# Sliding-window attention with a three-way maxout block: differences of hidden blocks issued later, normalising on VectorE, part of the weights' low parts on GpSimd

## The chip, the cores and the metric

The kernel runs on one core of one Trainium2 chip. A core has five engines, each with an instruction queue of its own that is worked off in order: PE (TensorE, matmuls; PEld are its weight loads), DVE (VectorE), ACT (ScalarE), POOL (GpSimd) and SP (SyncE, here only DMA issues). The metric is the device time of one execution in microseconds (us); less is better.

## The reference

q, k and v are 8 batches x 8 heads x 576 positions x 64; the block behind the attention has 4608 tokens, d_model 512 and d_ff 768.

```python
scores = scale * np.matmul(q, k.transpose(0, 1, 3, 2))
bias = slopes[:, None, None] * (-np.abs(rel).astype(np.float32))[None, :, :]
mask = (rel >= 0) & (rel < window)            # window = 128
scores = np.where(mask, scores + bias[None], -1000000000.0)
attn = np.exp(scores - np.max(scores, axis=-1, keepdims=True))
attn = attn / (np.sum(attn, axis=-1, keepdims=True) + 1e-09)
x = np.matmul(attn, v)                        # heads side by side: 4608 x 512
h = np.maximum(np.maximum(x @ w1, x @ w2), x @ w3)
return (h @ w_out).astype(np.float32)
```

## The kernel before

*Attention.* A task is one batch and one pair of heads, a step one block of 128 queries of a task (five blocks, the last of 64). `score` adds the bias on DVE (L289, with the row's minimum into `st`), and ACT takes the exponential into a tile `p` with the row sums (L293). `sums_of` adds 1e-9 to the sums (L302) and takes reciprocals (L305), both on DVE, for two blocks at a time. `normalise` (L312) multiplies each of the two heads' halves of `p` by the reciprocal of its row, on ACT. `turn` transposes `p` on PE (L321), ACT copies it out (L325, L334) and POOL cuts it into two triangles (L335, L339); `mix` multiplies with v (L361).

*The block behind it* is one level of a two-by-two fast matrix product in seven products of sums and differences of blocks (k = 0 to 6). A unit is one product k of one group g of 128 columns; each batch has 9 groups of the first layer (three matrices for each of three parts p of d_ff) and 2 groups of the last, 77 units. Matrices are split into a high part of reduced precision and the rest, the low part, and a product is three matmuls per 128 rows: six matmuls for a unit of the first layer, nine for one of the last (L510). `unit` takes the result out of PSUM: k below 3 by an ACT copy (L519), the others in `put` on DVE (L468, L473 to L476, L459) or ACT (L457, L470). Three PSUM banks go round, so that a unit needs the bank that was taken out three units earlier.

*Weights.* `preparing` reads twelve groups of weights once, converts them from words (L136 to L144), forms sums (L158), and splits each of the seven blocks of 256 columns in `part`: the high part on ACT (L168), the low part on DVE (L169). Groups 0 to 8 are stored to DRAM (L171, on SP's queue) and streamed back for each later batch (L221, on POOL's queue).

*Hidden blocks.* When a part p of the hidden layer is ready, `factors_h` forms its sums and differences on DVE (`sub`, L391) and splits them (`cut`): the high part by ACT (L387), the low part by POOL, or by DVE for p = 2 and k below 2 (L388). `factors_x` does the same for the attention's output. These calls are put into a list with a time in units by `later`, and `unit` calls what is due before its own matmuls.

*Order.* `at` gives each call a time in steps; the calls are recorded sorted by it. The units of a batch are spread over the steps of the next batch's attention. A scheduler then sets each engine's order from the recorded program, and buffers are few, so that a late instruction in one queue holds back all that stand behind it there.

Of the kernel before, what the change touches and what calls it, by code (L numbers as in the profile page):

```python
# [8 lines left out]
F32 = mybir.dt.float32  # L9
# [3 lines left out]
AF = mybir.ActivationFunctionType  # L13
ALU = mybir.AluOpType
# [15 lines left out]
def attention_maxout_kernel(  # L30
# [11 lines left out]
    nc = tc.nc  # L42
# [43 lines left out]
        out=prev, in_=prev, pattern=[[1, P]], compare_op=ALU.is_gt, fill=0.0,  # L86
# [59 lines left out]
    def blocks(g):  # L146

        (l0, h0), (l1, h1) = [[x.bitcast(F32) for x in words(g, j)] for j in range(2)]
        a, b = slice(0, W), slice(W, 2 * W)
        return l0[:, a], h0[:, b], h1[:, a], h1[:, b], l1[:, a], h0[:, a], l1[:, b], l0[:, b]  # L150
# [9 lines left out]
    def part(g, k):  # L160
        src = blocks(g)[k]
        if g < 9:
            if k in (0, 4):
                place(g, k // 4)
            t = wts[g, k // 4][:, k % 4]
        else:
            t = ow[k][:, g - 9]
        nc.scalar.copy(out=t[:, 0], in_=src)  # L168
        nc.vector.tensor_tensor(out=t[:, 1], in0=src, in1=t[:, 0].bitcast(F32), op=ALU.subtract)  # L169
        if g < 9 and k in (3, 6):  # L170
            nc.sync.dma_start(keep[g][k // 4], wts[g, k // 4].bitcast(F32))  # L171

    def place(n, a):
        wts[n, a] = wt_p.tile([P, 4 - a, 2, W], F32R, name=f"wt{a}")
# [8 lines left out]
    def preparing():  # L183
        fetch(0)
        fetch(1)
        for n, g in enumerate(g_order):
            for j in range(2):
                convert(g, j)
                yield
            sums(g)  # L190
            yield
            for k in range(7):
                while g < 9 and not ahead(g, k // 4):
                    yield True
                part(g, k)
                yield
            if n + 2 < NG:
                fetch(g_order[n + 2])
# [108 lines left out]
    def normalise(t, i):  # L307
        n = rows[i]
        st, two = stats[t, i // 2]
        for a, p in enumerate(two):  # L310
            for j in range(2):
                nc.scalar.activation(p[:n, j], p[:n, j], AF.Copy, scale=st[:n, 2, a, j:j + 1])  # L312

    def turn(s):
        pt = ps_t.tile([P, 2, 2, P], F32, name="pt")
# [63 lines left out]
    def later(when, what, *args):  # L379
        todo.append((when, what, args))  # L380
        todo.sort(key=lambda x: x[0])
# [3 lines left out]
    def split(out, src, e):  # L385
        hi, lo = out
        nc.scalar.copy(out=hi, in_=src)  # L387
        e.tensor_tensor(out=lo, in0=src, in1=hi.bitcast(F32), op=ALU.subtract)  # L388

    def sub(out, x, y):  # L390
        nc.vector.tensor_tensor(out=out, in0=x, in1=y, op=ALU.subtract)  # L391
# [28 lines left out]
    def factors_h(b, p, ij, when):  # L420
        b00, b01, b10, b11 = [hq.get((p, x)) for x in ((0, 0), (0, 1), (1, 0), (1, 1))]

        def cut(k, src):
            if p < 2:
                if p == 0:
                    hs[b, k] = hs_p.tile([P, 2, 2, C], F32R, name="hs")
                t = hs[b, k][:, p]
            else:
                if k in (0, 2, 4, 5):
                    hs[b, "at"] = hs_p.tile([P, 2, 2, C], F32R, name="hs2", bufs=4)  # L430
                t = hs[b, k, 2] = hs[b, "at"][:, k in (1, 3, 6)]
            split((t[:, 0], t[:, 1]), src, nc.vector if p == 2 and k < 2 else nc.gpsimd)

        if ij == (0, 0):
            t = hq["t", p] = t_p.tile([P, C], F32, name="t")
            sub(t, b01, b00)
            later(when, cut, 0, b00)
            later(when, cut, 1, t)
        elif ij == (1, 1):
            t = hq["t", p]  # L440
            later(when, sub, t, b11, t)
            later(when, sub, b01, b11, b01)
            later(when, cut, 2, t)
            later(when, cut, 3, b11)
        elif ij == (1, 0):
            t = hq["t", p]
            later(when, cut, 5, b01)
            later(when, cut, 4, b10)
            later(when, sub, b10, b10, t)
            later(when, cut, 6, b10)  # L450

    def put(b, g, ij, ps, e, when):
        i, j = ij
        if g >= 9:
            o = t_p.tile([P, C], F32, name="t")
            if e is None:
                nc.scalar.copy(out=o, in_=ps)  # L457
            else:
                nc.vector.tensor_tensor(out=o, in0=ps, in1=e, op=ALU.add)  # L459
            m = i * W + (g - 9) * P  # L460
            nc.sync.dma_start(outT[m:m + P, b * S + j * C:b * S + (j + 1) * C], o)
            return
        p, w = divmod(g, 3)
        if w == 0:
            hq[p, ij] = hq_p.tile([P, C], F32, name="hq")
        h = hq[p, ij]
        if w and e is None:
            nc.vector.tensor_tensor(out=h, in0=ps, in1=h, op=ALU.max)  # L468
        elif e is None:
            nc.scalar.copy(out=h, in_=ps)  # L470
        elif w:
            s = t_p.tile([P, C], F32, name="t")
            nc.vector.tensor_tensor(out=s, in0=ps, in1=e, op=ALU.add)  # L473
            nc.vector.tensor_tensor(out=h, in0=s, in1=h, op=ALU.max)  # L474
        else:
            nc.vector.tensor_tensor(out=h, in0=ps, in1=e, op=ALU.add)  # L476
        if w == 2:
            factors_h(b, p, ij, when + 1)
# [54 lines left out]
    for t, (b, hp) in enumerate(tasks):  # L533
        for i in range(NB):
            s = t * NB + i + shift[b]
            if i == LOAD_I and t + 2 < len(tasks):
                at(s - 0.4, load, t + 2)
            if i == NB - 1 and t + 1 < len(tasks):
                at(s - 0.4, load_v, t + 1)
            if i == 0 and 0 < t < NP:  # L540
                at(s - 1, slopes, t)
            c = s - (t * NB + i) % 2

            if s == c:
                at(c + LAG_T + 0.02, turn, t * NB + i)
                at(c + 0.03, products, t * NB + i)
            at(s + 0.04, score, t, i)
            if i % 2 or i + 1 == NB:
                at(s + 0.9, sums_of, t, i)
                at(s + 1.3, normalise, t, i)  # L550
            e = t * NB + next(min(e + 1, NB - 1) for e in GROUPS if e >= i)
            at(e - e % 2 + shift[b] + LAG_X + 0.01, mix, t, i)

    ready = [n_steps * (b + 1) - 2 + LAG_X + 0.05 + shift[b] for b in range(B)]
    when = ready[0]
    for b in range(B):
# [4 lines left out]
        for u in range(77 * b, 77 * b + 77):  # L561
            if u == 77 * b + 63 and b + 1 < B:
                when = max(when, ready[b + 1])
# [53 lines left out]
```

## Time and profile before

| | us |
|---|---|
| median of 3 runs | 849.85 (846.66 to 851.54) |
| the profiled execution | 846.03 |
| its span | 844.3 |
| PE busy | 780.3 (92%) |
| DVE busy | 570.0 (68%) |
| ACT busy | 544.5 (64%) |
| POOL busy | 310.3 (37%) |

All that follows is read from one profiled execution. Times are us from the start of the span unless marked ns. A row such as "A <- B" says that A's engine stood idle until B was done. A group's busy time leaves out overlaps, so it can be less than its count times its mean. Tile names stand as out<-in, with the program's numbers left out: `hq` are hidden blocks, `hs` their split parts and also the raw weights, `xk` and `xs` the same for the attention's output, `t` temporaries, `wt` and `ow` split weights, `ps_m` the PSUM banks of the units, `ps_s` those of the scores.

### The profile page before, as it was taken

How to read it: one execution, taken by the hardware profiler on the slowest of the kernel's cores; microseconds unless marked ns; L12 is line 12 of the kernel's file. 1: busy time of each engine (PE TensorE's matmuls, PEld its weight loads, DVE VectorE, ACT ScalarE, POOL GpSimd, SP SyncE). 2: the span in 40 equal slices, each digit the busy share in tenths (PEclk: the TensorE clock that was granted, in tenths of full speed). 3: DMA queues.
4: the chain of work that ended last, by engine and by line, in shares of the span. 5: the costliest groups of instructions: out<-in, count | busy, mean ns of one | idle time of the engine just before them, and what ended most of it. 6: DMA issues, size and time to landing. Idle time of an engine off the chain costs nothing.

```text
span 844.3 us, 17942 instructions
## 1 busy us (share of the span) xinstructions
PE 780.3 (92%) x6272; PEld 674.3 (80%) x6272; DVE 570.0 (68%) x1830; ACT 544.5 (64%) x1790; POOL 310.3 (37%) x544
## 2 busy tenths in 40 slices
PE   4767778799999999999999999999999999999997
PEld 2335666589888988888888988889888988889897
DVE  5788989996666845775557845775657846583552
ACT  6898888876666856676556756675657756642332
POOL 1212141442354415452345415451345415440431
PEclk9865989799999999999999999999999999999999
DMA  6742568673887558873787558873787557764851
GB/s 230 278 168 70 220 230 305 210 257 125 262 277 249 195 171 261 277 253 118 239 273 252 196 175 267 275 255 110 245 281 240 194 187 244 230 223 153 296 205 56
DMA packets 43401, 184.78 MB, mean 219 GB/s; under 512 B 4784, under 2 KB 13744, under 8 KB 34096
## 3 DMA queue, kind: packets, MB, share of 16 engines
q0 software_dynamic: 18144, 115.61, 41.7%
q1 hardware_dynamic: 25024, 67.97, 22.8%
q8 instruction: 49, 0.80, 0.4%
q14 instruction: 40, 0.33, 0.1%
q10 hardware_dynamic: 144, 0.07, 0.0%
HBM read 157.68 MB, written 25.95 MB: 217 GB/s over the span
## 4 chain that ended last, share of the span: by engine, by line
PE 68%; DVE 8%; issue 8%; POOL 6%; ACT 6%; DMA 3%; SPq 0%; POOLq 0%; ACTq 0%; DVEq 0%
PE ps_m L510 53%; PE ps_x L361 6%; PE ps_s L259 5%; PE pt L321 4%; POOL hs L388 3%; DMA wt<-keep 2%; POOL pp L339 1%; POOL pp L335 1%; ACT p L293 1%; ACT hs L387 1%; DVE hs L158 1%; DVE t L473 1%; DMA hs<-in_w_all 1%; DVE hs L144 1%; DVE xs L388 1%
## 5 line engine op out<-in xcount | busy, mean ns | idle before, releaser
L510 PE MATMUL ps_m<-xs,wt 128*128 128x288 f32 x3024 | 440.8, 302 | 19.9 <-DVE hq L476 7.6
L510 PEld LDWEIGHTS ps_m<-xs,wt 128*128 128x128 f32 x3024 | 414.6, 191 | 46.6 <-issue 12.2
L519 ACT COPY t<-ps_m 128x288 f32<-128x288 f32 x264 | 101.2, 392 | 92.3 <-PE ps_m L510 91.9
L335 POOL TENSOR_SCALAR_AFFINE_SELECT pp<-pr 128x256 f32<-128x256 f32 (+1 forms) x128 | 53.9, 421 | 263.0 <-ACT pr L334 175.9
L510 PE MATMUL ps_m<-hs,ow 128*128 128x288 f32 x1008 | 144.5, 299 | 3.2 <-POOL hs L388 2.4
L293 ACT ACTIVATE p<-s,st 128x128 f32<-128x128 f32 (+1 forms) x320 | 126.7, 399 | 27.9 <-DVE st L289 27.2
L510 PEld LDWEIGHTS ps_m<-hs,ow 128*128 128x128 f32 x1008 | 136.0, 188 | 9.6 <-POOL hs L388 5.9
L388 POOL TENSOR_TENSOR hs<-hq,hs 128x288 fp32r<-128x288 f32 x112 | 101.3, 914 | 88.3 <-ACT hs L387 88.1
L221 POOL DMA_DIRECT2D wt<-keep x126 | 69.8, 554 | 150.3 <-PE ps_m L510 148.8
L312 ACT ACTIVATE p<-p,st 128x128 f32<-128x128 f32 (+1 forms) x320 | 108.6, 399 | 20.6 <-DVE st L305 20.0
L289 DVE CUSTOM_DVE_ANT_0 s<-ps_s,bias 128x128 f32<-128x128 f32 (+1 forms) x300 | 77.5, 283 | 25.9 <-PE ps_s L259 19.0
L473 DVE TENSOR_TENSOR t<-ps_m,t 128x288 f32<-128x288 f32 x144 | 65.1, 453 | 43.5 <-PE ps_m L510 27.3
L361 PE MATMUL ps_x<-pp,v 128*64 128x256 f32 (+3 forms) x768 | 85.6, 338 | 7.3 <-POOL pp L335 6.6
L277 DVE COPY_PREDICATED ps_s<-prev,ps_s 128x256 f32<-128x256 uint8 x120 | 50.6, 421 | 56.9 <-PE ps_s L259 55.7
L259 PE MATMUL ps_s<-qk 64*64 64x192 f32 (+1 forms) x1080 | 71.3, 346 | 11.5 <-DVE st L289 7.4
L321 PE MATMUL pt<-ident,p 128*128 128x128 f32 (+1 forms) x320 | 62.0, 295 | 17.3 <-ACT p L312 15.2
L387 ACT CAST hs<-hq 128x288 fp32r<-128x288 f32 x120 | 50.3, 433 | 39.0 <-DVE hq L474 26.0
L361 PEld LDWEIGHTS ps_x<-pp,v 128*64 128x64 f32 (+1 forms) x768 | 46.7, 140 | 35.1 <-POOL pp L335 11.8
L321 PEld LDWEIGHTS pt<-ident,p 128*128 128x128 f32 (+1 forms) x320 | 37.2, 145 | 42.7 <-ACT p L312 20.9
L474 DVE TENSOR_TENSOR hq<-t,hq 128x288 f32<-128x288 f32 x144 | 67.4, 475 | 2.7
L259 PEld LDWEIGHTS ps_s<-qk 64*64 64x64 f32 x1080 | 40.1, 141 | 26.9 <-issue 13.2
L293 ACT ACTIVATION_READ_ACCUMULATOR p<-s,st 128x1 f32 (+1 forms) x320 | 61.5, 192 | 0.0
(56 smaller groups left out, 719.2 us busy)
## 6 DMA issues: line engine op xcount, KB each, us to landing
wt<-keep POOLq DMA_DIRECT2D x63, 1024.0 KB, 7.2
wt<-keep POOLq DMA_DIRECT2D x63, 768.0 KB, 4.6
qk<-in_qk SPq DMA_DIRECT2D x31, 576.0 KB, 5.8
hs<-in_w_all SPq DMA_DIRECT2D x24, 512.0 KB, 6.6
v<-in_v SPq DMA_DIRECT2D x32, 320.0 KB, 4.8
keep<-wt SPq DMA_DIRECT2D x9, 1024.0 KB, 4.7
outT<-t SPq DMA_DIRECT2D x64, 144.0 KB, 1.8
keep<-wt SPq DMA_DIRECT2D x9, 768.0 KB, 5.2
```

Of the source, the lines that this page charges most:

```text
L221: nc.gpsimd.dma_start(wts[n, a], keep[n % 9][a])
L259: nc.tensor.matmul(ps[j][d:d + D, o:o + k1 - k0], lhsT=qkt[t][j * D:(j + 1) * D, 0, q0:q0 + D], rhs=qkt[t][j * D:(j + 1) * D, 1, k0:k1], s ...
L289: nc.vector.tensor_tensor_reduce(out=s[:n], in0=ps[j][:n, P:2 * P], in1=(bias if i else bias0)[:n, 2 * hp + j, :], scale=-0.125, scalar=3. ...
L293: nc.scalar.activation(p[:n, j], s[:n], AF.Exp, bias=st[:n, 0, a, j:j + 1], scale=-1.0, accum_out=st[:n, 1, a, j:j + 1])
L312: nc.scalar.activation(p[:n, j], p[:n, j], AF.Copy, scale=st[:n, 2, a, j:j + 1])
L321: nc.tensor.transpose(out=pt[:, a, j, :n], in_=p[:n, j], identity=ident[:n, :n])
L361: nc.tensor.matmul(x[j * D:(j + 1) * D, c:c + e - a], lhsT=vv[:n, i, j * D:(j + 1) * D], rhs=w[:n, j].rearrange("p a b -> p (a b)")[:, a:e ...
L388: e.tensor_tensor(out=lo, in0=src, in1=hi.bitcast(F32), op=ALU.subtract)
L473: nc.vector.tensor_tensor(out=s, in0=ps, in1=e, op=ALU.add)
L474: nc.vector.tensor_tensor(out=h, in0=s, in1=h, op=ALU.max)
L510: nc.tensor.matmul(ps, lhsT=lt, rhs=rt, start=i == 0 and k in (0, 1, 4), stop=i == len(pairs) - 1, skip_group_check=True,)
L519: nc.scalar.copy(out=e, in_=ps)
```

## The change

Three edits. The multiplications of `normalise` go from ACT to DVE. Of each group's seven low parts of weights, those of k = 1, 2, 3 and 5 are computed by POOL, the other three stay on DVE. In `factors_h`, what follows the block (1, 1) comes two units later for p below 2, and the last difference and its split come five units later for every p.

```diff
-        nc.vector.tensor_tensor(out=t[:, 1], in0=src, in1=t[:, 0].bitcast(F32), op=ALU.subtract)
+        e = nc.gpsimd if k in (1, 2, 3, 5) else nc.vector
+        e.tensor_tensor(out=t[:, 1], in0=src, in1=t[:, 0].bitcast(F32), op=ALU.subtract)
...
-                nc.scalar.activation(p[:n, j], p[:n, j], AF.Copy, scale=st[:n, 2, a, j:j + 1])
+                nc.vector.tensor_scalar(
+                    out=p[:n, j], in0=p[:n, j], scalar1=st[:n, 2, a, j:j + 1], scalar2=None, op0=ALU.mult
+                )
...
             t = hq["t", p]
+            when += 2 * (p < 2)
             later(when, sub, t, b11, t)
...
-            later(when, sub, b10, b10, t)
-            later(when, cut, 6, b10)
+            later(when + 5, sub, b10, b10, t)
+            later(when + 5, cut, 6, b10)
```

Lines of the changed kernel from 170 on carry numbers one to four higher: L169 becomes L170, L302 and L305 become L303 and L306, L312 becomes L313, L388 and L391 become L391 and L394, L468 to L476 become L472 to L480, L510 becomes L514.

How this moves instructions, at three places. DVE in a middle batch, where the first part of the hidden layer has just been taken out and the next group's first evacuations come (L476, then L480: hq from a bank of PSUM; `hq<-hq,t` is the last difference); before:

```order
L289 ISA s,st<-ps_s,bias_115 128x128
L289 ISA st 128x1
L391 TENSOR_TENSOR hq<-hq,t 128x288
L476 TENSOR_TENSOR hq<-ps_m_5666,t 128x288
L476 TENSOR_TENSOR hq<-ps_m_5754,t 128x288
L302 TENSOR_SCALAR st<-st 64x2
L476 TENSOR_TENSOR hq<-ps_m_5655,t 128x288
L305 RECIPROCAL st<-st 64x2
```

and after:

```order
L290 ISA s,st<-ps_s,bias_115 128x128
L290 ISA st 128x1
L480 TENSOR_TENSOR hq<-ps_m_5658,t 128x288
L303 TENSOR_SCALAR st<-st 64x2
L394 TENSOR_TENSOR hq<-hq,t 128x288
L480 TENSOR_TENSOR hq<-ps_m_5750,t 128x288
L306 RECIPROCAL st<-st 64x2
L480 TENSOR_TENSOR hq<-ps_m_5647,t 128x288
L313 TENSOR_SCALAR p<-p,st 64x128 x2
```

One evacuation passes the difference, the sum L303 passes it too, and two multiplications follow the third evacuation.

DVE where the last part of the hidden layer is split, beside the first group of the last layer (L459, then L463, are its evacuations); before:

```order
L459 TENSOR_TENSOR t<-ps_m_6396,t 128x288
L388 TENSOR_TENSOR xs<-xk_6091,xs 128x576
L391 TENSOR_TENSOR hq<-hq,t 128x288
L388 TENSOR_TENSOR xs<-xk_6091,xs 128x576
L459 TENSOR_TENSOR t<-ps_m_6477,t 128x288
L388 TENSOR_TENSOR xs<-xk_5424,xs 128x576
L459 TENSOR_TENSOR t<-ps_m_6380,t 128x288
L391 TENSOR_TENSOR xk_6091<-xk_6091,xt 128x2x288
```

and after:

```order
L313 TENSOR_SCALAR p<-p,st 64x128
L463 TENSOR_TENSOR t<-ps_m_6396,t 128x288
L391 TENSOR_TENSOR xs<-xk_6088,xs 128x576
L313 TENSOR_SCALAR p<-p,st 64x128
L391 TENSOR_TENSOR xs<-xk_6088,xs 128x576
L463 TENSOR_TENSOR t<-ps_m_6474,t 128x288
L391 TENSOR_TENSOR xs<-xk_5424,xs 128x576
L463 TENSOR_TENSOR t<-ps_m_6380,t 128x288
L394 TENSOR_TENSOR xk_6088<-xk_6088,xt 128x2x288
L394 TENSOR_TENSOR hq<-hq,t 128x288
```

The difference of the hidden block goes from behind the first evacuation to behind the third and behind the difference of `xk`, and two multiplications stand between.

POOL at the start, where the masks of the attention (L335 and L339, then L338 and L342) come first; before:

```order
L99 AFFINE_SELECT bias_115<-bias 128x256 x4
L335 AFFINE_SELECT pp<-pr 128x2x128
L339 AFFINE_SELECT pp<-pr 128x2x128
L335 AFFINE_SELECT pp<-pr 128x2x128
L339 AFFINE_SELECT pp<-pr 128x2x128
```

and after:

```order
L99 AFFINE_SELECT bias_115<-bias 128x256 x4
L170 TENSOR_TENSOR wt_285<-hs_182,wt_285 128x256
L170 TENSOR_TENSOR wt_226<-hs_182,wt_226 128x256
L170 TENSOR_TENSOR wt_226<-hs_184,wt_226 128x256 x2
L338 AFFINE_SELECT pp<-pr 128x2x128
L342 AFFINE_SELECT pp<-pr 128x2x128
```

The four low parts of the first group stand ahead of the masks, and further groups follow in the same way.

## The prediction

> **What bounds the kernel now.** I read busy time cut into stages first, then PE's waits stage by stage, then the place of the longest wait in order of time. The stages; the columns are the stretch in us, its length, busy us with the count of instructions for each engine, TensorE's granted clock, and the DMA share with GB/s.
>
> ```profile
> 0.00:75.00 75.00, 47.46 (x314) 23.17 (x315) 56.55 (x225) 62.84 (x214) 16.98 (x42) 0.78 0.59 209
> 75.00:195.00 120.00, 100.80 (x730) 82.22 (x729) 113.42 (x340) 97.88 (x299) 35.89 (x55) 0.87 0.62 223
> ...
> 378.79:473.22 94.43, 92.76 (x786) 82.33 (x785) 61.34 (x203) 60.51 (x206) 38.92 (x70) 1.00 0.69 228
> ```
>
> There are two kernels in one. From about 195 us on, every batch takes 94.4 us of which PE is busy 92.8: PE is the bound, and the idle on top is 1.7 us per batch. Before that PE is not the bound. To 75 us ACT (63 of 75) and DVE (57 of 75) share the work of the first batch's attention; from 75 to 195 us DVE is busy 113.4 of 120, so DVE sets the pace while weights are prepared. The change touches both stages, with different prices. Now what PE waited for, first between 20 and 195 us, then from 190 us to the end (total us, times, longest):
>
> ```profile
> PE pt L321 <- ACT p L312: 10.9, 8, 3.1
> ...
> PE ps_m L510 <- ACT t L519: 5.1, 3, 4.3
> ...
> PE ps_m L510 <- DVE hq L476: 7.0, 5, 1.4
> ```
>
> The last row says how little the PE-bound part can give: it is the largest of PE's waits there, 7.0 us over 650, one of 1.4 us per batch. This is it, in order of time (DVE, then POOL, then PE; start, us, count, idle before and its releaser):
>
> ```profile
> 330.31 0.29 DVE L289 CUSTOM_DVE_ANT_0 s<-ps_s,bias 128x128 f32<-128x128 f32 x1 [0.71 <-ACT p L293]
> 332.24 0.46 DVE L391 TENSOR_TENSOR hq<-hq,t 128x288 f32<-128x288 f32 x1 [1.63 <-POOL hs L388]
> 332.62 0.82 DVE L476 TENSOR_TENSOR hq<-ps_m,t 128x288 f32<-128x288 f32 x2
> 333.35 0.73 DVE L302 TENSOR_SCALAR st<-st 64x2 f32<-64x2 f32 x1
> ...
> 330.65 1.55 POOL L388 TENSOR_TENSOR hs<-hq,hs 128x288 fp32r<-128x288 f32 x2
> ...
> 333.12 2.12 PE L510 MATMUL ps_m<-xs,wt 128*128 128x288 f32 x14 [1.41 <-DVE hq L476]
> ```
>
> The difference L391 overwrites a block that POOL's low part still reads, so it waits for POOL until 332.2; two evacuations L476 stand behind it on DVE, and PE stands 1.41 us for the first.
>
> **The change, part by part.** The prices, from the view of groups by shape (busy us, mean ns); the last row is of 76 to 195 us alone:
>
> ```profile
> L312 ACT ACTIVATE p<-p,st 128x128 f32<-128x128 f32 x256 | 86.0, 398 | 6.8 <-DVE st L305 6.2
> L169 DVE TENSOR_TENSOR wt<-hs,wt 128x256 fp32r<-128x256 f32 x63 | 26.8, 443 | 2.3 <-ACT wt L168 2.1
> L169 DVE TENSOR_TENSOR ow<-hs,ow 128x256 fp32r<-128x256 f32 x21 | 8.5, 429 | 1.0 <-ACT ow L168 1.0
> L302 DVE TENSOR_SCALAR st<-st 64x2 f32<-64x2 f32 x32 | 24.4, 761 | 5.7 <-ACT p L293 5.2
> L302 DVE TENSOR_SCALAR st<-st 128x4 f32<-128x4 f32 x64 | 12.7, 198 | 14.0 <-ACT p L293 12.9
> L141 DVE TENSOR_SCALAR hs<-hs 128x512 int32<-128x512 int32 x24 | 10.4, 452 | 0.0
> ...
> L388 POOL TENSOR_TENSOR hs<-hq,hs 128x288 fp32r<-128x288 f32 x14 | 12.9, 927 | 18.5 <-ACT hs L387 18.5
> ```
>
> Low parts. Of 84 low parts, 4 of 7 per weight group leave DVE: 48, at 0.42 us (26.8 + 8.5 over 84), so -20 us of DVE, all of it before 195 us. On POOL there is no row for this shape; the nearest is POOL's low part of 128x288 at 0.93, so 256/288 of it, 0.82 us, bounds 0.45 (the DVE price) to 0.93: +39 us of POOL on the 17.0 + 35.9 that it is busy up to 195 us. POOL's share rises from 27% to 47%. In POOL's queue the masks L335 and L339 now stand behind groups of four low parts. On SP the stores of finished weights wait for POOL where they waited for DVE, and loads of later groups stand behind them; these loads are issued two groups ahead, which hides that, at worst a few tenths.
>
> Normalising. 320 activations leave ACT at about 0.33 us (86.0 over 256), 40 per batch: -13 us of ACT per batch. DVE gets 40 multiplications of 128x128 with a scalar per row. No row shows one. Below it is L302 of 4 columns, 0.198 us, above L141 of 512 columns, 0.452, both plain tensor_scalars. I take 0.22, close to the lower one because the width is nearer to it. Up to 195 us two batches are normalised: 80 times 0.22, +18 us of DVE (16 to 36).
>
> [...]
>
> So far DVE gains 2 us and ACT 26 up to 195 us. What the plain counts leave out is that DVE and POOL stand in each other's way. This row of DVE, and two of POOL beside it:
>
> ```profile
> 352.52 3.32 DVE L302 TENSOR_SCALAR st<-st 64x2 f32<-64x2 f32 x1
> ...
> 352.72 0.83 POOL L388 TENSOR_TENSOR hs<-t,hs 128x288 fp32r<-128x288 f32 x1
> 353.50 2.31 POOL L388 TENSOR_TENSOR hs<-hq,hs 128x288 fp32r<-128x288 f32 x3
> ```
>
> A tensor_scalar over two columns took 3.32 us, until POOL's four instructions were over; the same one at 333.35, shown above, took 0.73 us beside one POOL instruction. That is why the 64x2 group has a mean of 761 ns. Instructions with two operands in SBUF lengthen too. In a dense stretch of the weights' work, POOL ran five instructions from 149.60 to 153.29 without a gap, the first and last of them below; beside them two L141 and an L158 of DVE had these means:
>
> ```profile
> 149.60 0.61 POOL L335 TENSOR_SCALAR_AFFINE_SELECT pp<-pr 128x256 f32<-128x256 f32 x1 [9.02 <-ACT pr L325]
> 152.07 1.22 POOL L388 TENSOR_TENSOR hs<-hq,hs 128x288 fp32r<-128x288 f32 x1
> ...
> L141 DVE TENSOR_SCALAR hs<-hs 128x512 int32<-128x512 int32 x2 | 1.2, 625 | 0.0
> L158 DVE TENSOR_TENSOR hs<-hs 128x256 f32<-128x256 f32 x1 | 1.0, 1016 | 0.0
> ```
>
> Against the group's 452 and against the 0.43 of a tensor_tensor of the same width (L169) that is 0.35 + 0.58 us lost beside 3.7 us of POOL, 0.25 us for each.
>
> [...]
>
> The size of it here. At 0.25 us for each us of POOL, 39 us more of POOL would cost DVE 10 us; the stretch is a dense one, so that is near the upper end, and I take 8 (3 to 13). The new multiplications meet POOL 47 times in 100; a meeting costs half a POOL instruction, 0.4 us, which for 80 of them is 15 us; since four stand in a row and only the first ones meet POOL by chance, I take half, 7 (0 to 15). DVE's sum up to 195 us is -20 + 18 + 8 + 7, +13 us (-1 to +44).
>
> What of that is on the path. To 75 us DVE has 18 us of idle and ACT falls from 63 to about 50 us, so I put the half of the 13 that falls there at 0. From 75 to 195 us DVE has 6.6 us of idle and the other half, 6.5 us, cannot hide; against it stand PE's waits for ACT above (10.9 and 5.1 us), which a freer ACT shortens. I take +4 for the start (-6 to +10).
>
> The PE-bound part. Per batch DVE gets 9 us and some stalls on 61.3 of 94.4: hidden by 33 us of idle, and nothing of ACT's gain shows, since ACT was at 60.5. What counts are evacuations that come late, since PE needs a bank again two units later, and a unit of six matmuls is about 0.82 us (8.09 us over 59 in the last fence of this part, times 6). At the wait of 333.12 the new order puts one evacuation ahead of the difference, and the L302, the difference and a second evacuation behind it. The first can then start at 330.6 (330.31 + 0.29), but the second still waits for POOL's 332.2 and the difference behind it, and ends at 333.1; PE would want it one unit after 331.71 (333.12 - 1.41), at 332.53, so that 0.57 us of wait would be left if POOL came when it does now. It comes later: on DVE four multiplications stand now ahead of the difference t<-hq,t whose low part opens this run of POOL, beside POOL's two low parts of the first blocks, and each can lose half an instruction; that shifts the run by about 1 us and gives the wait back. I take 0 (-1.4 to +1.0 per batch).
>
> Second place: the last block of the third group of units. Its difference and low part were done here:
>
> ```profile
> 381.62 0.45 DVE L391 TENSOR_TENSOR hq<-hq,t 128x288 f32<-128x288 f32 x1
> 383.95 0.45 DVE L459 TENSOR_TENSOR t<-ps_m,t 128x288 f32<-128x288 f32 x1
> 384.31 0.89 DVE L391 TENSOR_TENSOR xk<-xk,xt 128x576 f32<-128x576 f32 x1
> ...
> 382.61 0.80 POOL L388 TENSOR_TENSOR hs<-hq,hs 128x288 fp32r<-128x288 f32 x1 [1.53 <-ACT hs L387]
> 384.18 8.09 PE L510 MATMUL ps_m<-hs,ow 128*128 128x288 f32 x59
> ```
>
> PE uses it in the third nine of that run of 59, from the 25th matmul on: 384.2 + 24 x 0.137 = 387.5. In the new order the difference comes after the third evacuation (now at 383.95) and after the other difference (384.31), so at about 385.2 or, with two multiplications that meet POOL, 386. From its start to the end of its low part it is 1.8 us in these rows (381.62 to 383.41), so it is ready at 387.0 to 387.8. That nearly holds; I take +0.2 per batch (0 to 1.0).
>
> Over seven batches: +1.5 us (-10 to +14). The tail has no attention, and its waits are for DMA: 0.
>
> Sum: +4 + 1.5 = +5.5. The profiled execution took 846.0 us for a span of 844.3, 3.8 under the median of 849.85; put on the median, 855.4.
>
> **The rivals.** First, faster: ACT, not DVE, sets the first 195 us. For it: ACT is the busier one to 75 us, and PE's largest wait up to 195 is for the activations that leave ACT. If half of the 16 us of waits for ACT go, DVE's stalls stay at the lower ends, and the 7.0 us of waits at L476 vanish by the one evacuation that stands ahead, it is -6 - 7: 837 us. Against it: DVE is at 95% in the stage that is 120 us long.
>
> Second, nothing to see: the stalls are half of what I count, the start comes out even, and the later difference stands on DVE only one evacuation further on than before, so that the change of place does little. 850 us.
>
> Third, clearly slower: a run of POOL like that of 352.52 holds multiplications that stand ahead of evacuations once per batch. It decides once a stall exceeds about 1 us, the room between the end of an evacuation and the matmul that needs the bank. 2 us over seven batches and +4 at the start: 868 us. For it: that row. Against it: the one long stall of today hid behind other matmuls, and few of a batch's twelve groups of multiplications meet a run that long.
>
> **How the numbers follow.** My forecast, DVE's stalls in the start and little change after, 0.42, with a range of its own of 850 to 862; of that 0.09 lies within 0.5% of the median, which is about what a measurement of this kernel can tell from no change, 4.2 us. The faster rival 0.31, even 0.15, clearly slower 0.12. So faster 0.31, same 0.24, slower 0.45. The bounds of the terms reach from -16 to +24; half of each outer rival is enough for 8 in 10: 834 to 868.
>
> **What would show it.** Right: between 75 and 195 us DVE stays above 93% with ACT under 75%, the stage is longer by some us, tensor_scalars L303 and L313 have means well above 0.25 us, and POOL's low part L170 takes 0.8 us. In the batches, the wait of PE for the evacuation L480 stays near a microsecond. Wrong: a first stage up to 75 us that is clearly shorter (then ACT was the bound), the wait at L480 gone, or multiplications at 0.22 us throughout. A 94.4 us batch that grows by over 1 us is the third rival.

## The result and the profile after

The changed kernel takes 872.35 us (median of 4 runs, 870.35 to 874.49) against 848.8 for the kernel before on the same chip: 1.0276 of its time, 95% interval 1.023 to 1.0322. That is slower by 23.6 us and above the range of the prediction (868).

The profiled execution has a span of 872.8 us. Its stages, with the columns of the first view of before; the last row is one middle batch:

```profile
0.00:75.00 75.00, 44.66 (x266) 20.86 (x266) 53.12 (x213) 46.09 (x152) 24.98 (x50) 0.82 0.55 196
75.00:195.00 120.00, 94.47 (x607) 72.81 (x608) 110.24 (x331) 79.99 (x236) 58.76 (x79) 0.80 0.52 183
...
515.73:611.32 95.59, 93.78 (x787) 82.51 (x786) 70.46 (x243) 49.61 (x166) 40.27 (x69) 1.00 0.69 225
```

PE does 266 matmuls in the first 75 us where it did 314, and 607 in the next 120 where it did 730, while ACT, freed of its multiplications, falls from 63 to 46 us and from 98 to 80. DVE is not busier than before in either stretch; there is just less done in it. A stretch of fixed length hides that, so all that follows goes by three marks in the program: the begin of batch 0's units (the first matmul of L510, now L514), the end of those units, and the distance between the begins of later batches. (The marks between batches are taken at the same count of matmuls in every run, 0.9 us behind the first matmul of the next batch.) From before to after the begin goes from 74.4 to 85.8 us, the end from 205.7 to 227.2, and a later batch from 94.4 us to between 95.4 and 96.1. So 21.5 us lie in the start, 11.4 ahead of the units and 10.1 in batch 0's units, and 6.9 in the rest. These are the 28.5 us between the two profiled executions; that of before is 2.8 us under its median and that of after 2.1 above, so some 5 of them are spread between executions.

PE's waits after, first to 75 us, then from 75 to 200, then the rest (total us, times, longest):

```profile
PE pt L324 <- DVE p L313: 12.6, 8, 6.5
PE ps_x L364 <- POOL pp L338: 7.3, 4, 3.1
...
PE ps_m L514 <- DVE t L477: 8.7, 5, 4.0
...
PE ps_m L514 <- POOL hs L391: 7.6, 8, 1.4
...
PE ps_m L514 <- DVE hq L480: 2.9, 4, 0.7
```

Over the whole span the wait for the normalised weights that stood at ACT stands at DVE, hardly larger in sum (15.2 us before, 15.7 after). But up to the begin of the units it grew by 4.7 us, and the wait for POOL's masks by 5.7. Before, up to 75 us:

```profile
PE pt L321 <- ACT p L312: 10.4, 4, 4.2
...
PE ps_x L361 <- POOL pp L335: 4.1, 5, 1.5
```

and after, up to 85.81 us:

```profile
PE pt L324 <- DVE p L313: 15.1, 9, 6.5
PE ps_x L364 <- POOL pp L338: 9.8, 7, 3.1
```

In the batches the wait for the evacuation fell from 7.0 to 2.9 us, and a wait for POOL's low parts, 2.1 before, took its place with 7.6. The prices over the whole span:

```profile
L313 DVE TENSOR_SCALAR p<-p,st 128x128 f32<-128x128 f32 x256 | 88.2, 392 | 1.1
L170 POOL TENSOR_TENSOR wt<-hs,wt 128x256 fp32r<-128x256 f32 x36 | 29.7, 839 | 43.5 <-ACT wt L168 43.4
L313 DVE TENSOR_SCALAR p<-p,st 64x128 f32<-64x128 f32 x64 | 19.6, 339 | 0.4
L170 DVE TENSOR_TENSOR wt<-hs,wt 128x256 fp32r<-128x256 f32 x27 | 12.6, 473 | 0.0
...
L170 POOL TENSOR_TENSOR ow<-hs,ow 128x256 fp32r<-128x256 f32 x12 | 9.5, 812 | 7.3 <-ACT ow L168 7.3
```

A multiplication is busy for 0.34 us on average ((88.2 + 19.6)/320) over the whole span, stalls included: the median is 0.28, and the longest took 3.61 us (756.92 to 760.53) beside four low parts of POOL (L391, 757.38 to 760.44). POOL's 48 low parts took 39.2 us at 0.84 and 0.81 each.

### The profile page after: what moved, and what is told of

It reads as the page before. It is cut to its first block, busy times and chain, and to the rows that moved or that the text cites. A ratio compares the mean times of both kernels' runs of the same rounds, so it can differ in the third digit from the quotient of the medians.

```text
span 872.8 us, 17969 instructions
## 1 busy us (share of the span) xinstructions
PE 794.8 (91%) x6272; PEld 679.9 (78%) x6272; DVE 638.0 (73%) x2102; ACT 458.1 (52%) x1470; POOL 359.4 (41%) x592
## 4 chain that ended last, share of the span: by engine, by line
PE 49%; DVE 17%; POOL 8%; issue 7%; DMA 5%; ACT 4%; SPq 0%; ACTq 0%; POOLq 0%; DVEq 0%
PE ps_m L514 37%; POOL hs L391 5%; PE ps_x L364 4%; PE ps_s L260 4%; DMA wt<-keep 3%; PE pt L324 3%; DVE p L313 3%; DVE hq L478 2%; POOL pp L342 2%; DMA hs<-in_w_all 2%; DVE t L477 2%; DVE hs L158 1%; DVE t L394 1%; POOL pp L338 1%; DVE ps_s L278 1%
## 5 line engine op out<-in xcount | busy, mean ns | idle before, releaser
L514 PE MATMUL ps_m<-xs,wt 128*128 128x288 f32 x3024 | 444.5, 303 | 26.2 <-DVE t L477 9.4
L514 PEld LDWEIGHTS ps_m<-xs,wt 128*128 128x128 f32 x3024 | 416.1, 192 | 56.0 <-DVE t L477 15.3
L523 ACT COPY t<-ps_m 128x288 f32<-128x288 f32 x264 | 103.0, 395 | 124.1 <-PE ps_m L514 122.0
L514 PE MATMUL ps_m<-hs,ow 128*128 128x288 f32 x1008 | 145.7, 299 | 8.5 <-POOL hs L391 7.6
L514 PEld LDWEIGHTS ps_m<-hs,ow 128*128 128x128 f32 x1008 | 136.2, 188 | 16.1 <-POOL hs L391 12.1
L338 POOL TENSOR_SCALAR_AFFINE_SELECT pp<-pr 128x256 f32<-128x256 f32 (+1 forms) x128 | 58.2, 455 | 216.9 <-ACT pr L337 116.7
L222 POOL DMA_DIRECT2D wt<-keep x126 | 69.9, 555 | 145.6 <-PE ps_m L514 145.0
L391 POOL TENSOR_TENSOR hs<-hq,hs 128x288 fp32r<-128x288 f32 x112 | 100.1, 903 | 70.1 <-ACT hs L390 67.7
L313 DVE TENSOR_SCALAR p<-p,st 128x128 f32<-128x128 f32 (+1 forms) x320 | 107.8, 381 | 1.5
L364 PE MATMUL ps_x<-pp,v 128*64 128x256 f32 (+3 forms) x768 | 88.9, 342 | 10.7 <-POOL pp L338 10.4
L477 DVE TENSOR_TENSOR t<-ps_m,t 128x288 f32<-128x288 f32 x144 | 64.6, 452 | 31.0 <-PE ps_m L514 29.0
L260 PE MATMUL ps_s<-qk 64*64 64x192 f32 (+1 forms) x1080 | 73.4, 347 | 11.9 <-DVE st L290 7.3
L364 PEld LDWEIGHTS ps_x<-pp,v 128*64 128x64 f32 (+1 forms) x768 | 48.1, 143 | 38.8 <-issue 14.2
L324 PE MATMUL pt<-ident,p 128*128 128x128 f32 (+1 forms) x320 | 62.4, 298 | 17.0 <-DVE p L313 15.7
L478 DVE TENSOR_TENSOR hq<-t,hq 128x288 f32<-128x288 f32 x144 | 71.4, 502 | 2.2
L342 POOL TENSOR_SCALAR_AFFINE_SELECT pp<-pr 128x256 f32<-128x256 f32 (+1 forms) x128 | 65.5, 512 | 0.0
```

Source lines behind the costliest of these rows:

```text
L260: nc.tensor.matmul(ps[j][d:d + D, o:o + k1 - k0], lhsT=qkt[t][j * D:(j + 1) * D, 0, q0:q0 + D], rhs=qkt[t][j * D:(j + 1) * D, 1, k0:k1], s ...
L313: nc.vector.tensor_scalar(out=p[:n, j], in0=p[:n, j], scalar1=st[:n, 2, a, j:j + 1], scalar2=None, op0=ALU.mult)
L324: nc.tensor.transpose(out=pt[:, a, j, :n], in_=p[:n, j], identity=ident[:n, :n])
L342: nc.gpsimd.affine_select(out=w[:n, :, 0, :n], in_=r[:n, a, :, :n], pattern=[[0, 2], [1, n]], compare_op=ALU.is_ge, fill=0.0, base=0, chan ...
L364: nc.tensor.matmul(x[j * D:(j + 1) * D, c:c + e - a], lhsT=vv[:n, i, j * D:(j + 1) * D], rhs=w[:n, j].rearrange("p a b -> p (a b)")[:, a:e ...
L514: nc.tensor.matmul(ps, lhsT=lt, rhs=rt, start=i == 0 and k in (0, 1, 4), stop=i == len(pairs) - 1, skip_group_check=True,)
```

## The experiments

Marks of every run, from its profiled execution; the ratio to the kernel before is from all its runs, with the 95% interval. Where a multiplication of p stands is the column to watch. Among the kernels that leave it on ACT the begin differs by 2 us and the length by 6, so a single difference of 2 or 3 us proves little.

| run | p multiplied by | begin, us | batch 0's units to batch 1's, us | a later batch, us | median, us | ratio |
|---|---|---|---|---|---|---|
| before | ACT | 74.4 | 131.1 | 94.4 to 94.5 | 848.8 to 850.1 | 1 |
| after | DVE | 85.8 | 141.3 | 95.4 to 96.1 | 872.35 | 1.0276 (1.023 to 1.0322) |
| norm_only | DVE | 82.3 | 143.8 | 95.5 to 96.2 | 873.65 | 1.0297 (1.0275 to 1.0319) |
| low_only | ACT | 76.7 | 130.1 | 94.5 | 848.37 | 0.9989 (0.9975 to 1.0003) |
| later_only | ACT | 76.2 | 136.5 | 93.6 to 94.2 | 849.49 | 0.9994 (0.9976 to 1.0013) |
| low_later | ACT | 75.0 | 132.8 | 93.7 to 93.9 | 849.4 | 0.9996 (0.9972 to 1.002) |
| norm_b0 | DVE in batch 0 | 82.7 | 132.9 | 94.5 | 856.5 | 1.0099 (1.0078 to 1.0119) |
| norm_late | DVE from batch 2 | 74.9 | 131.2 | 95.5 to 95.7 | 854.29 | 1.0067 (1.0043 to 1.0091) |
| doubled | ACT, idle ones on DVE | 74.9 | 142.1 | 96.2 to 96.5 | 869.4 | 1.0246 (1.0219 to 1.0272) |
| no_norm | nobody | 79.6 | 136.8 | 95.6 to 95.8 | 865.26 | 1.0204 (1.0166 to 1.0241) |
| norm_soon | DVE, due earlier | 83.5 | 142.7 | 98 to 99.5 | 891.25 | 1.0479 (1.0447 to 1.0511) |
| norm_due3 | DVE, due later | 79.5 | 145.6 | 96.0 to 96.1 | 873.5 | 1.0287 (1.0259 to 1.0315) |
| norm_tt | DVE, in another form | 79.7 | 148.8 | 95.0 to 95.1 | 874.04 | 1.0288 (1.0262 to 1.0314) |
| later_b1 | ACT | 76.3 | 132.5 | 93.6 to 93.7 | 845.46 | 0.9951 (0.9933 to 0.9969) |
| bias_first | ACT | 75.9 | 132.6 | 94.4 to 94.5 | 849.15 | 0.9997 (0.9986 to 1.0008) |
| mirror | DVE, idle ones on ACT | 79.4 | 144.1 | 95.6 | 871.52 | 1.0258 (1.024 to 1.0276) |
| filled | nobody, idle ones on ACT | 72.4 | 133.4 | 94.8 to 95.0 | 848.56 | 0.9999 (0.998 to 1.0018) |

**Which of the three edits.** The edits of the diff one at a time (norm_only the multiplications, low_only the low parts, later_only the differences), and the changed kernel with the multiplications back on ACT (low_later):

> The kernel before with the multiplications of normalise on DVE, nothing else changed. In the changed kernel the units of batch 0 begin 11.4 us later than before (85.8 against 74.4) and last 10.2 us longer (141.3 against 131.1), and each later batch is about 1.2 us longer. Theory N (the multiplications stand in DVE's queue in the dense start, and the transposes on PE wait for them): most of the 21 us at the start come back here, 865 to 870, batches 95 to 96 us. Theory L (the low parts on POOL do it, by the masks and the loads that stand behind them): 848 to 856. Theory J (only together, multiplication and POOL on the shared path): 850 to 857 with multiplications at about 0.28 us in place of the 0.38 of the changed kernel.

> The kernel before with the low parts k = 1, 2, 3, 5 of the weights on POOL, nothing else changed. Theory L: 862 to 870, all of it before the end of batch 0's units, batches at 94.4 us as before. Theory N: 845 to 853, as DVE is freed of 20 us. Theory J: 847 to 856.

> The kernel before with the later differences alone. Theory G (the last block of the third group of units comes too late for the first group of the last layer, where PE waits 0.9 us for POOL in a changed batch): batches of 95 to 95.5 us, the 1.41 us wait of PE for the evacuation halved, 849 to 856. Rival (the difference's place alone is harmless, the lateness comes from the multiplications that stand ahead of it): batches of 93 to 94.4 us, 840 to 849. The start to the end of batch 0's units stays at 205.7 us within 2 us by either.

> The changed kernel with the multiplications of normalise back on ACT, so the low parts on POOL and the later differences. Theory N: within 4 us of the kernel before. Theory L: 862 to 872. Theory J: 848 to 858, with the later differences' share on top.

Normalising on DVE is the whole loss, and the other two edits together cost and gain nothing: theory N, though norm_only's 873.65 us lies 4 us above the range that N gave. Later_only's batches are those of the rival. What neither of its theories allowed is that batch 0's units end at 212.9 us, 7 us later than before; that takes back what the batches gain. The other half of the question is why 48 low parts less on DVE gain nothing. Up to the end of batch 0's units, the kernel before, in its two stages:

```profile
0.00:74.42 74.42, 46.88 (x313) 22.59 (x313) 55.97 (x223) 62.27 (x212) 16.98 (x42) 0.78 0.59 211
74.42:205.69 131.27, 112.07 (x819) 92.98 (x820) 119.66 (x364) 104.19 (x320) 38.73 (x60) 0.88 0.60 215
```

and the kernel with the low parts alone on POOL:

```profile
0.00:76.69 76.69, 51.21 (x313) 26.52 (x313) 52.54 (x205) 62.29 (x211) 30.74 (x60) 0.80 0.57 204
76.69:206.90 130.21, 113.05 (x819) 92.73 (x820) 116.23 (x334) 104.21 (x321) 63.17 (x91) 0.92 0.61 217
```

POOL took 38.2 us more. DVE has 48 instructions less, worth 20 us, and is busy 168.8 us in place of 175.6: 13 of the 20 did not come off. By the sums of their durations, the instructions that stayed on DVE are some 9.6 us longer beside POOL. The rest is overlap: in the rows of DVE an instruction starts 0.07 to 0.08 us before the one ahead of it ends (332.62 against 332.24 + 0.46 us, in the prediction's rows), so not all of a duration is gained when an instruction goes. The stage of 130 us has 3.4 us less of DVE's time and is 1.1 us shorter, which is within what kernels of one kind differ by.

**Where normalising costs.**

> The kernel before with normalise on DVE for batches 2 to 7 alone; batches 0 and 1, whose attention lies in the start where the weights are prepared, stay on ACT. Theory S (the start pays, and a later batch about 1 us, as in the run with normalise alone, where batches took 95.5 in place of 94.46 us): the end of batch 0's units at 205 to 208 us, later batches 95.3 to 95.7, 852 to 857. Rival (the order of the later batches, set from the beginning of the program, pays too): above 860.

> The kernel before with normalise on DVE for batch 0 alone. In the run with normalise alone the units of batch 0 began 7.9 us later than before (82.3 against 74.4) and lasted 12.7 us longer. Theory Q (DVE's queue is the bound from the first weights on, each multiplication is paid where it stands): units of batch 0 begin at 80 to 84 us and last 131 to 135 us, total 855 to 860. Theory C (to 75 us DVE has a quarter of idle time and only batch 1's multiplications, in the stage after it, cost): begin at 74 to 77 us, total 848 to 853.

```diff
-                nc.scalar.activation(p[:n, j], p[:n, j], AF.Copy, scale=st[:n, 2, a, j:j + 1])
+                if t >= 2 * NP:   # norm_late; norm_b0: t < NP
+                    nc.vector.tensor_scalar(out=p[:n, j], in0=p[:n, j], scalar1=st[:n, 2, a, j:j + 1], ...)
+                else:
+                    nc.scalar.activation(p[:n, j], p[:n, j], AF.Copy, scale=st[:n, 2, a, j:j + 1])
```

Theory S holds in the first run and the numbers of theory Q in the second: 5.4 us for batches 2 to 7 (854.3 against 848.9), and 7.6 for batch 0 (856.5 against 848.9), nearly all of it ahead of the units. The 11 that are left of 24 would belong to batch 1, in the stage of batch 0's units; that is a subtraction, since no run has batch 1 alone. There seem to be two different costs in the start, then, ahead of the units and in them.

**Is it DVE's time, or the way that p takes?** DVE's load without moving anything:

> The kernel before, normalise stays on ACT, and DVE gets a multiplication of the same size beside each one, behind the reciprocals, from a constant into a tile that nobody reads; the biases of all heads are formed at once at the beginning, so that a tile is free for it. Nothing waits for the added multiplications but DVE's queue. Theory Q (DVE's time in the start is what is paid): the end of batch 0's units 15 to 25 us later than 205.7, total 862 to 875. Theory C2 (the chain is paid: exponential, sums, reciprocal, multiplication, transpose, with the multiplication now waiting in DVE's queue): 849 to 856, as nothing on the chain is moved.

```diff
                 nc.scalar.activation(p[:n, j], p[:n, j], AF.Copy, scale=st[:n, 2, a, j:j + 1])
+                nc.vector.tensor_scalar(
+                    out=dist[:n], in0=ident[:n], scalar1=st[:n, 2, a, j:j + 1], scalar2=None, op0=ALU.mult
+                )
```

```profile
0.00:74.93 74.93, 48.21 (x313) 22.79 (x313) 63.02 (x261) 62.90 (x211) 18.25 (x42) 0.75 0.58 205
74.93:217.15 142.22, 116.71 (x823) 97.37 (x820) 130.75 (x415) 105.20 (x322) 39.36 (x60) 0.87 0.57 201
```

Each theory holds in one stage. Ahead of the units DVE carried 7 us more (63.0 against 56.0) and the begin did not move, since its idle time took them. In the units DVE was busy 130.8 us in place of 119.7, its idle time stayed (11.5 against 11.6 us), and the stage became 11 us longer: there DVE's time is paid one for one in this run. (In the changed kernel it is 8.8 us more of DVE and 10.2 us more of the stage.) The end of the stage came 11.5 us later than before, not the 15 to 25 of theory Q, but the total is Q's. A later batch pays for load alone as well: 96.2 to 96.5 us, more than in norm_only.

**What is paid ahead of the units.** I had named the place behind the conversion of weights in DVE's queue:

> The kernel with normalise alone on DVE (873.65 in its run), and normalise is due directly behind the sums (0.91 of a step) in place of 0.4 of a step later. Theory P (in the first 80 us DVE has idle time, and what is paid is the place of the multiplications behind the conversion of weights in DVE's queue, since transposes, copies and that conversion wait for each other in turn): the units of batch 0 begin at 75 to 80 us in place of 82.3, total 864 to 872. Theory Q2 (what is paid is the hop from ACT's exponential over DVE to PE whatever the place): begin at 81 to 84, total 871 to 876.

> The same kernel with normalise due 1.3 steps later than in the run with normalise alone (at 2.6 of a step, the transposes are due at 4). Theory P: the place moves behind still more of the conversion, or past it, so the begin of batch 0's units moves by 2 us or more to either side of 82.3, and the later batches change as well. Theory Q2: begin at 81 to 84, 871 to 876.

```diff
-                at(s + 1.3, normalise, t, i)
+                at(s + 0.91, normalise, t, i)   # norm_soon; norm_due3: s + 2.6
```

In norm_due3 two blocks of every second task are transposed before they are multiplied; the amount of work is the same.

Theory P fell on the first of these: 0.4 of a step earlier left the begin where it was (83.5), as Q2 has it. The total is 15 us above Q2's range, since a later batch costs 2 to 4 us more, which I haven't traced. The later place gave 2.8 us at the begin, which P allows and Q2 does not, and lost 1.8 of them in the units; its total is Q2's. So neither theory covers both. The next run was the one without any multiplication:

> The kernel before without the multiplications of normalise on any engine (the weights of the attention stay unnormalised). Theory Q: ACT is relieved of 26 us and the chain loses a link, but DVE keeps its work, so 842 to 850, with the end of batch 0's units at 198 to 206 us. Theory C2: the chain is shorter by 1.4 us for each pair of blocks plus the wait for ACT, 825 to 840. By either a later batch stays at 94.4 us within 0.8.

Less work, and 16 us slower, with later batches 1.2 us longer: neither theory allowed for that. Then the same with ACT's queue filled again, the turned-round doubled run, and their common base:

> The kernel before with p not multiplied at all, and as many multiplications of the same size from a constant into a tile that nobody reads left in ACT's queue. The run without any multiplication began batch 0's units at 79.6 us and took 865. Theory O: begin at 73 to 77 us, units of batch 0 in 128 to 134, total 842 to 850, so that added idle work on ACT makes the kernel some 16 us faster. Theory H: the shorter chain shows here, 66 to 73 us. Rival R (the unmultiplied numbers, or chance of the order, made that run slow): begin at 78 us or more.

> As the run with doubled multiplications, but turned round: DVE multiplies p, and ACT does as many multiplications of the same size from a constant into a tile that nobody reads. Both engines carry the load that they carried there; only who makes p is changed. All kernels so far with the multiplications in ACT's queue began batch 0's units at 74.4 to 76.7 us, all without them there at 79.5 to 85.8, with the multiplications at three places in DVE's queue and even with none at all. Theory O (what is paid in the first 80 us is what ACT does in the place of the multiplications: it runs conversions of weights ahead of exponentials and copies, and stands in them): begin at 74 to 77.5 us. Theory H (the hop ACT, DVE, PE is paid): begin at 80 to 85. By both the units of batch 0 last 138 to 146 us, since DVE carries the multiplications, and a later batch is 95.3 to 96.5.

> The kernel before, with the biases of all heads formed at once at the beginning and nothing else changed: the common part of the two runs with idle multiplications. Any theory: within 0.5% of the kernel before, the begin of batch 0's units at 74 to 77 us and their length at 129 to 137.

```diff
-                nc.scalar.activation(p[:n, j], p[:n, j], AF.Copy, scale=st[:n, 2, a, j:j + 1])
+                nc.scalar.activation(dist[:n], ident[:n], AF.Copy, scale=st[:n, 2, a, j:j + 1])
```

This is filled; mirror adds the multiplication of p on DVE, and both, like doubled, form all biases at the beginning, which is all that bias_first does:

```diff
-                at(s - 1, slopes, t)
...
-    slopes(0)
+    for hp in range(NP):
+        slopes(hp)
```

Idle work on ACT makes the kernel without multiplications 17 us faster (865.3 to 848.6). In the profiled executions the begin is 7.2 us earlier, batch 0's units are 3.4 us shorter and the rest 4.8. The total is that of theory O, and rival R fell; but the begin, 72.4 us, lies just outside O's range and inside that of theory H, so the shorter chain may have a share in it. What ACT waits for up to 85 us differs most; without multiplications:

```profile
ACT xk L368 <- PE ps_x L359: 6.4, 4, 3.7
ACT pr L332 <- PE pt L319: 6.3, 3, 3.1
ACT p L293 <- DVE st L289: 4.8, 2, 4.2
ACT pr L323 <- PE pt L319: 4.5, 3, 2.0
```

and filled:

```profile
ACT p L293 <- DVE st L289: 5.5, 3, 4.4
...
ACT pr L325 <- PE pt L321: 0.2, 1, 0.2
```

Copies out of PSUM, `pr` and `xk`, stand in ACT's in-order queue ahead of exponentials, and ACT stands 17 us at them until PE has caught up, while the exponentials behind them, which PE will need, are not begun. The scheduler placed them so. Without multiplications the conversion of the next group (L136) comes ahead of the exponentials of the fourth block:

```profile
16.03 0.71 ACT L136 ACTIVATE hs<-hs 128x512 int32<-128x512 uint32 x1
...
17.91 0.71 ACT L136 ACTIVATE hs<-hs 128x512 int32<-128x512 uint32 x1
18.48 0.42 ACT L293 ACTIVATE p<-s,st 128x128 f32<-128x128 f32 x1
```

filled, it comes after those and two more pairs:

```profile
18.11 0.42 ACT L293 ACTIVATE p<-s,st 128x128 f32<-128x128 f32 x1
...
22.41 0.39 ACT L293 ACTIVATE p<-s,st 128x128 f32<-128x128 f32 x1
...
23.09 0.67 ACT L136 ACTIVATE hs<-hs 128x512 int32<-128x512 uint32 x1
```

That is how ACT differs; it is not shown to be what the 7.2 us are paid for. Up to the begin of the units, without multiplications and then filled:

```profile
0.00:79.58 79.58, 56.58 (x314) 25.58 (x315) 54.68 (x222) 53.56 (x176) 18.55 (x42) 0.80 0.55 197
0.00:72.35 72.35, 48.86 (x317) 23.57 (x317) 56.88 (x230) 62.72 (x216) 17.61 (x42) 0.74 0.62 217
```

PE is idle for 23.0 us in the one and 23.5 in the other. What is longer without multiplications is its busy time, by 7.7 us for no more matmuls: they are slower (the last section shows one shape). Whether ACT's order made them slower, or the two only came together, no run here separates. In norm_only it is the other way round: PE is busy for 46.8 us up to the begin, as before (46.9), and idle for 35.5 in place of 27.5. ACT stands at the copies there too, 16.4 us up to 80 us against 3.4 before.

Mirror divides the 8 us of the begin: with ACT's load as in the doubled run and only the maker of p changed it begins 4.5 us later (79.4 against 74.9), between the ranges of the two theories. That is what the hop over DVE costs, ACT to DVE to PE, and it is about twice what kernels with p on ACT differ by. It does not show at p itself: up to the begin PE waits 10.8 us for p in mirror and 11.2 in doubled, while its waits for DVE's work on the scores (L289) go from 5.7 to 8.4 us and those for POOL's masks from 4.1 to 5.3. With ACT's queue emptied as well the begin is another 2.9 us later (82.3). That is near what kernels of one kind differ by, and norm_due3 and norm_tt, whose ACT is as empty, begin at 79.5 and 79.7, so a share of theory O in the changed kernel is not shown. In the changed kernel the begin is 3.5 us later still (85.8), with POOL's low parts ahead of the masks, for which PE waits 9.8 us there and 6.1 in norm_only; that step was not tested alone.

**The form of the multiplication.**

> The kernel with normalise alone on DVE, and each block's two multiplications written as one tensor_tensor of 128x256 with the reciprocals broadcast along the row. Theory T (a tensor_scalar that meets POOL waits until POOL is done, a tensor_tensor only slows): the busy time of normalise falls from 0.33 us for each 128 columns to about 0.21, with no instruction above 1.5 us, and the time to the end of batch 0's units falls by 4 us or more, total 862 to 869. Rival (both forms wait alike, and the bare time sets the rest): 869 to 876, with single instructions above 2 us.

```diff
-            for j in range(2):
-                nc.vector.tensor_scalar(out=p[:n, j], in0=p[:n, j], scalar1=st[:n, 2, a, j:j + 1], ...)
+            nc.vector.tensor_tensor(
+                out=p[:n], in0=p[:n], in1=st[:n, 2, a].unsqueeze(2).broadcast_to([n, 2, P]), op=ALU.mult
+            )
```

```profile
L311 DVE TENSOR_TENSOR p<-p,st 128x256 f32<-128x256 f32 (+1 forms) x160 | 88.7, 575 | 1.3
```

In norm_only the group of tensor_scalars is busy 98.7 us, so 128 columns fell from 0.31 to 0.28 us and not to 0.21; single instructions reach 3.67 us here and 3.61 there. The rival holds by its numbers (874.04 us, and 3.67 where it says above 2); what POOL did beside the instruction of 3.67 us is not shown.

**A version that beats both.**

> The kernel before with the later differences alone, from batch 1 on; batch 0's stay where they were. In the run with later differences a later batch took 93.6 to 94.2 us in place of 94.46, and its batch 0 was 5 us longer in the profiled execution. Theory G2 (the gain of about 0.7 us per batch is of the later place, and the start lost by it): the end of batch 0's units at 205 to 207, 844 to 847. Rival (the start's time varies with the order whatever is changed): 847 to 851.

The edit is `when += 2 * (p < 2 and b > 0)` and `when + 5 * (b > 0)` in the kernel before. It takes 845.46 us, 0.5% less than before, as G2 has it, by 0.8 us on each later batch. Its begin and end of batch 0's units (76.3, 209.0) are no better than in the other kernels with ACT, so that part of G2 isn't shown.

## Why the prediction was wrong

*The step that failed* is "What of that is on the path": 0 for what falls up to 75 us, and +4 (-6 to +10) for the start as a whole. Measured: +11.4 ahead of batch 0's units and +10.1 in them. The batches, +6.9 against +1.5, lie inside their range.

*DVE's sum* came out: +13 us predicted up to the end of the start, 175.6 to 190.2 measured, +14.6. That is partly luck. The multiplications alone add 14.2 us of busy time (norm_only, 189.9), where 25 were forecast with their stalls. The low parts alone take 6.9 away (low_only), where 12 were forecast, and the two together are 7.3 us more than their sum. The price of a low part on POOL was right: 39 us forecast, 39.2 measured. So was that of DVE's stalls beside it, 8 (3 to 13), some 9.6 by durations in low_only.

*From 75 us* the reading "DVE sets the pace" was right, and the doubled run shows it. The slip was to set a gain from a freer ACT against DVE's 6.5 us. In this stage PE's wait for ACT's evacuation did fall (5.1 us at L519, 2.0 at L523), but that for DVE's `t` went from 1.6 to 8.7 (L473, L477). DVE is busy 128.4 us in this stage of the changed kernel in place of 119.7: low parts left it, but the multiplications and the stalls weigh more, and its queue was already full: of the stage of 131.3 us before it was idle for 11.6.

*To 75 us* the 0 was wrong. DVE's idle time hides load, as I said (doubled), but not a change of the maker of p, which costs 4.5 us of the begin in mirror. In the changed kernel PE's idle time up to the begin goes from 27.5 to 35.0 us, with the longer waits for p and for POOL's masks shown above, and its busy time from 46.9 to 50.9. The other 7 of the 11.4 us stay open between POOL's low parts, ACT's new order and slower matmuls. "ACT falls from 63 to about 50 us" was no gain at this place: it fell to 46. The prediction compared the order of DVE and of POOL; ACT's, from which the multiplications went, it did not look at.

*The batches.* The wait at the evacuation: 0 forecast (-1.4 to +1.0). PE waits 1.41 us there before and 0.72 after, one unit later, so -0.7. It is 0.63 in the three kernels with the later differences and p on ACT, whose later batches are 0.3 to 0.8 us shorter. The one evacuation that stands ahead did help, and only the second waits. The last block of the third group: +0.2 forecast (0 to 1.0); PE waits 0.89, where it waited 0.18 before. This is the place in the changed kernel, DVE, ACT, POOL, PE:

```profile
599.85 0.45 DVE L394 TENSOR_TENSOR hq<-hq,t 128x288 f32<-128x288 f32 x1
...
600.54 0.43 ACT L390 CAST hs<-hq 128x288 fp32r<-128x288 f32 x1
...
600.89 0.92 POOL L342 TENSOR_SCALAR_AFFINE_SELECT pp<-pr 128x256 f32<-128x256 f32 x1
601.78 0.79 POOL L391 TENSOR_TENSOR hs<-hq,hs 128x288 fp32r<-128x288 f32 x1
...
602.62 3.57 PE L514 MATMUL ps_m<-hs,ow 128*128 128x288 f32 x25 [0.89 <-POOL hs L391]
```

The difference comes when it was forecast (84.1 us after the batch's begin; 83.6 to 84.4 by the working). Its high part is done at 600.97, but POOL is at the masks until 601.8: 2.7 us from the difference to the low part's end, in place of 1.8. *Normalising in the batches* was put at nothing, hidden by 33 us of DVE's idle: norm_late shows 1.05 us per batch. About half of it can be seen in norm_only: ACT stands 2.58 us for a difference of DVE that was late, the evacuation is behind it, and PE waits 0.54:

```profile
598.03 0.95 DVE L394 TENSOR_TENSOR xk<-xk,xt 128x576 f32<-128x576 f32 x1
...
599.01 0.68 ACT L390 CAST xs<-xk 128x576 fp32r<-128x576 f32 x1 [2.58 <-DVE xk L394]
...
600.47 0.67 ACT L522 COPY t<-ps_m 128x288 f32<-128x288 f32 x2
...
600.90 0.79 PE L513 MATMUL ps_m<-hs,ow 128*128 128x288 f32 x4 [0.54 <-ACT t L522]
```

The end of batch 0's units to the end of the last is 635.3 us before and 642.2 after, +6.9 against +1.5 (-10 to +14).

*The rivals.* The first, that ACT sets the start, fell: ACT was freed and the start became longer. The third named a POOL run that holds a tensor_scalar ahead of evacuations; its price was too low and its place wrong for the changed kernel, but no_norm shows such a case in a late batch:

```profile
581.88 2.40 DVE L302 TENSOR_SCALAR st<-st 64x2 f32<-64x2 f32 x1
581.93 0.81 POOL L386 TENSOR_TENSOR hs<-t,hs 128x288 fp32r<-128x288 f32 x1
...
582.69 1.56 POOL L386 TENSOR_TENSOR hs<-hq,hs 128x288 fp32r<-128x288 f32 x2
...
584.52 0.40 ACT L293 ACTIVATE p<-s,st 128x128 f32<-128x128 f32 x1 [1.87 <-DVE st L289]
...
586.04 0.39 ACT L517 COPY t<-ps_m 128x288 f32<-128x288 f32 x1
...
586.48 0.79 PE L508 MATMUL ps_m<-hs,ow 128*128 128x288 f32 x4 [1.26 <-ACT t L517]
```

A sum over two columns takes 2.40 us, to 584.28, beside three instructions of POOL that end at 584.25; exponentials wait for DVE behind it, an evacuation waits behind them, and PE waits 1.26 us.

*The signs named.* DVE above 93% from 75 to 195 us: 92%. ACT below 75%: 67%. Multiplications above 0.25 us, POOL's low part at 0.8: so. The sums L303 are not: 0.19 us over four columns, and 0.33 over two, where they took 0.76 before. The wait at L480 near a microsecond: 0.7. The batch grew by about 1 to 1.6 us, which was the sign of the third rival, though by other waits than it named.

## What to carry to other kernels

An engine that gets lighter is not yet an engine that gets sooner: where a scheduler fills the room, look at that engine's new order for copies and conversions that stand in front of what others wait for. In this kernel DVE's idle time ahead of the units hid load (doubled: 7 us more of DVE, the begin at 74.9 for 74.4) but not a hop (mirror: 79.4), so price a step that moves to another in-order queue twice, by its time where that queue is full and by its wait where it is not. To tell the two apart, put the same work on the new engine without moving anything, and then idle work on the old one. And when a begin moves, split it into PE's idle and PE's busy time before naming a wait.

## What the runs showed that was not expected

The kernel without any multiplication became 17 us faster by idle work on ACT, as told above. And TensorE's speed was not told by the granted clock alone: from 20 to 30 us it reads 1.00 in both these kernels, yet a matmul of the same shape took 551 ns without and 348 with the idle work. Without:

```profile
L259 PE MATMUL ps_s<-qk 64*64 64x192 f32 x12 | 2.7, 551 | 0.0
```

and filled:

```profile
L259 PE MATMUL ps_s<-qk 64*64 64x192 f32 x12 | 1.6, 348 | 0.0
```

What made the same matmul slower in the one is not shown: no run here changes that by itself. So the 7.7 us of longer matmuls told above stay without a cause.
